# An attention scan with two expert layers: another order of the first pieces and loads, and other engines for the bonus and the low parts

## The chip, the core and the metric

The kernel runs on one core of one Trainium2 chip. The metric is the device time of one execution in microseconds (us). TensorE multiplies matrices, VectorE, ScalarE and GpSimd (POOL in the rows) work on elements, SyncE (SP) issues the transfers from and to HBM.

## The reference

Four sequences of 768 tokens, 8 heads of 48 columns. First a linear attention with a decaying state and a bonus `u` for the current token:

```
for t in range(S):
    cur = einsum('bhd,bhe->bhde', u[None] * kt, vt)
    y[:, :, t] = einsum('bhd,bhde->bhe', rt, state + cur)
    state = wt[..., None] * state + einsum('bhd,bhe->bhde', kt, vt)
```

Its 3072 rows of 384 go through a dense layer, `(max(h, 0) + alpha * min(h, 0)) @ w_out` with `h = x @ w_in` and 2048 inner columns, and then through eight experts of 1024 inner columns. Each row goes to the one expert whose normalised embedding has the largest product with it, and is scaled by its softmax weight.

## The kernel before

The tokens are cut into 24 tiles of 128 rows, tile n being chunk n // 4 of sequence n % 4, and three tiles make a block. The attention of a tile is written as eight pieces, `ATT[0..7]`, named `a<piece>.<tile>` in the table `PLAN`:

- `a0` (`att_p0`): a scan over the decays (L274), its inverse, and k times the result (L278), all on VectorE. `a1`: the second scan (L281), a square of the decays on ScalarE for a check (L283), and the bonus `att_u`, r times k times u on GpSimd (L289, L290).
- `a6` (`att_r`): r times the second scan (L295); from tile 4 on also the old state times its decay on GpSimd. `a7` (`att_d`): the bonus summed by head (L320) and multiplied with v (L322, tile `dv`).
- `a2`: k turned by TensorE (L330) and copied by ScalarE (`Kt`). `a3`: the scores of each head (L340), copied to `A` by ScalarE (L343) and masked by GpSimd (L344).
- `a4`: the new state (L354, L358, L360) and `y` (L366 and L369 on TensorE, L371 on VectorE, which adds `dv`). `a5`: `y` turned (L383) and split into a high part `xh` (ScalarE, L384) and a low part `xl` (VectorE, L385).

Matrices are multiplied as fp32r products of high and low parts, three for each product. The weights of the dense layer come as 64-bit words in 16 groups, `c<step>.<group>`: even groups are of w_in, odd ones of w_out. Step 0 is a shift on ScalarE (L197), step 1 two bit operations on VectorE (L199, L200), step 2 the high part on ScalarE (L211), step 3 the low part. The low part is one instruction on VectorE (L223), but for w_in's groups 2 to 5 (that is c4, c6, c8, c10, the list `LO_PE`) it is formed by TensorE (L219, L220) and copied by ScalarE (L221). `p0` and `p1` multiply w_out with the expert embeddings (`wt`, `wq`, L243 to L260). `s` normalises these embeddings (L879 to L886, tiles `en`, `ep`, `enT`) and casts the triangle `mf` to `trib`, and `w` is a run of idle products that keep TensorE busy.

`PLAN` is the order in which all engines get these pieces before the main loop. Then T counts 16 steps for each block: `l1` forms inner column group f = T mod 16 (nine products into `h_ps`, L408; then `m` on ScalarE and VectorE, L412 and L413, `gh`, L416, and `gl`, L422), `l2` takes the group of T - 2 to the outputs (L432). A step of block 0 also converts: step 0 of group T + 4, step 1 of T + 3, step 3 of T + 2. The pieces of a later tile begin at a T from the tables `AT1` and `AT`, and follow at distances `LAGS`. Each engine takes its instructions in exactly this order. There are two buffers for `h_ps`, and three PSUM buffers (`ps_a`) which the attention, the turned weights and the low parts share in turn. `LOADS` is the order of the first transfers, all on one queue of SyncE; a transfer is issued only when the eighth before it has landed.

Of the kernel before, what the change touches and what calls it, by code (L numbers as in the profile page):

```python
# [77 lines left out]
LOADS = [(0, "w"), "e", "id", (0, "rk"), "m", (0, "n"), "u", (1, "w"), (1, "rk"), (1, "n"), 0, (2,), 1, 2, 3]  # L78
PLAN = "a0.0 a1.0 s w6 a6.0 a2.0 a7.0 a3.0 a0.1 a1.1 a6.1 a4.0 a2.1 a7.1 a5.0 a3.1 c0.0 a0.2 a1.2 a6.2 a4.1 a2.2 a7.2 c1.0 c2.0 a5.1 a3.2 c0.1 c1.1 c3.0 c0.2 a4.2 c2.1 p0.0 c0.3 c1.2 a5.2 c3.1 c2.2"
# [15 lines left out]
def tile_main(ctx, tc, keep, x2d, tbl, att, w_in, w_out, alpha, u_row, u_col, emb, tau, w1, w2, cst, out):  # L95
# [95 lines left out]
    def conv(q, kind, g):  # L191

        t = stage[kind, g]
        lw, hw = t[:, :, 0], t[:, :, 1]
        lf = lw.bitcast(F32)
        if q == 0:
            ACT.activation(out=lf, in_=lw.bitcast(U32), func=AF.Copy, scale=-0.936 * 2.0 ** -51, bias=-2.0)  # L197
        elif q == 1:
            DVE.scalar_tensor_tensor(out=lw, in0=hw, scalar=3, in1=lw, op0=ALU.logical_shift_left, op1=ALU.bitwise_or)  # L199
            DVE.scalar_tensor_tensor(out=lw, in0=hw, scalar=0x3FFFFFFF, in1=lw, op0=ALU.bitwise_or, op1=ALU.bitwise_and)  # L200
        else:
            h, g0 = divmod(g, NG // 2)
            if kind == "in":
                hi, lo = (w[:, :, g0 * GW:(g0 + 1) * GW] for w in win[h])
            else:
                if h == len(wout):
                    wout_half()
                hi, lo = (w[:, g0 * GF:(g0 + 1) * GF, 0:DM] for w in wout[h])
            f3 = lf.rearrange("p (a b) -> p a b", a=(KD if kind == "in" else GF))
            if q == 2:  # L210
                ACT.activation(out=hi, in_=f3, func=AF.Copy, scale=-1.0)  # L211
            else:
                if (kind, g) in LO_PE:
                    m = 512 // hi.shape[2]
                    for a in range(0, hi.shape[1], m):
                        n = min(m, hi.shape[1] - a)
                        p = ps_a.tile([128, n, hi.shape[2]], F32, tag="a", name="lo_ps")
                        for b in range(n):
                            PE.matmul(out=p[:, b, :], lhsT=ident, rhs=f3[:, a + b, :], start=True, stop=False)  # L219
                            PE.matmul(out=p[:, b, :], lhsT=identr, rhs=hi[:, a + b, :], start=False, stop=True)  # L220
# [124 lines left out]

    def att_p4(n):
        c, b = divmod(n, B)
        r, v = rT(n, 0), nat(n, 2)
        if c < NCH - 1:
            up = ps_a.tile([128, HP, D], F32, tag="a", name="u_ps")  # L350
            for h in range(H):
                i = h % 2
                q = slice(64 * i, 64 * i + D)
                PE.matmul(out=up[q, h // 2, :], lhsT=Kt[:, h // 2, q], rhs=v[:, D * h:D * h + D], start=True, stop=True)  # L354
            for i in range(2):
                q = slice(64 * i, 64 * i + D)
                if c:
                    DVE.tensor_tensor(out=st[b][q], in0=up[q], in1=sbd[n % 2][q, :, D * i:D * i + D], op=ALU.add)  # L358
                else:
                    ACT.activation(out=st[b][q], in_=up[q], func=AF.Copy)  # L360
# [438 lines left out]
    if True:  # L799
        mf = sp.tile([128, 128], F32, tag="y", name="mf")  # L800
        for l in LOADS:
            if l == "e":
# [53 lines left out]
        def run(kind, *a):  # L856
# [474 lines left out]
```

## Time and profile before

| | us |
|---|---|
| median of 3 runs | 828.03 (827.75 to 828.66) |
| the profiled execution | 822.78 |
| its span, first to last instruction | 820.8 |
| TensorE busy | 788.3 (96%) |
| VectorE busy | 586.2 (71%) |
| ScalarE busy | 435.5 (53%) |
| GpSimd busy | 309.8 (38%) |

The shares are means over the whole span, in which the first 125 us, with the weights' conversion, differ from the rest. Durations below are from the profiled execution, whose time lies 5.25 us under the median.

### The profile page before, as it was taken

What the parts mean: (1) busy time and instruction counts of PE and PEld (TensorE: products, weight loads), DVE (VectorE), ACT (ScalarE), POOL (GpSimd) and SP (SyncE); (2) the same over time, 40 slices, a digit from 0 to 9 for tenths busy, and PEclk for the clock granted to TensorE, in tenths of its full rate; (3) what the DMA queues carried; (4) which work ended last, traced back from release to release, by engine and by line L of the source; (5) the groups of instructions that cost most, each with busy time, mean ns of one, the idle gap of its engine ahead of it and who ended that gap; (6) DMA issues with size and microseconds to landing.
All of it is one profiled execution on the core that took longest, in us unless ns stands there. A gap on an engine that the chain in (4) does not pass through costs nothing. (4 is left out here: it accounts for less than half of the span.)

```text
span 820.8 us, 16378 instructions
## 1 busy us (share of the span) xinstructions
PE 788.3 (96%) x6408; PEld 754.1 (92%) x6408; DVE 586.2 (71%) x1230; ACT 435.5 (53%) x845; POOL 309.8 (38%) x376
## 2 busy tenths in 40 slices
PE   6689999999999999999999999998899999999996
PEld 4579989999999999999999999897899999999996
DVE  6898886687586586676777674647987677768662
ACT  3667755345335444444533533436556676767662
POOL 4213322224124124124214212144466776767731
PEclk9689999999999999999999999999999999999998
DMA  8755512113324313113113100046756787676740
GB/s 316 257 164 210 178 69 88 68 53 114 123 82 149 123 58 98 69 68 97 70 68 97 69 1 30 31 168 203 183 207 210 272 272 261 223 278 225 257 174 32
DMA packets 31047, 117.26 MB, mean 143 GB/s; under 512 B 5693, under 2 KB 12829, under 8 KB 28145
## 3 DMA queue, kind: packets, MB, share of 16 engines
q0 software_dynamic: 13952, 59.86, 22.1%
q1 hardware_dynamic: 17008, 56.28, 20.0%
q8 instruction: 52, 0.85, 0.5%
q14 instruction: 35, 0.28, 0.2%
HBM read 101.79 MB, written 15.51 MB: 143 GB/s over the span
## 5 line engine op out<-in xcount | busy, mean ns | idle before, releaser
L412 ACT ACTIVATE m<-h_ps,al_sb 128x384 f32<-128x384 f32 x128 | 74.2, 580 | 125.9 <-PE h_ps L408 124.3
L413 DVE TENSOR_TENSOR m<-h_ps,m 128x384 f32<-128x384 f32 x128 | 71.0, 555 | 91.3 <-ACT m L412 89.9
L416 ACT ACTIVATE gh<-m 128x384 fp32r<-128x384 f32 x128 | 67.2, 525 | 113.3 <-DVE m L413 113.3
L422 DVE TENSOR_TENSOR gl<-m,gh 128x384 fp32r<-128x384 f32 x128 | 81.4, 636 | 36.2 <-ACT gh L416 36.1
L344 POOL TENSOR_SCALAR_AFFINE_SELECT A<-A 128x512 f32<-128x512 f32 x48 | 30.0, 648 | 178.0 <-ACT A L343 178.0
L685 POOL DMA_INDIRECT raw<-in_w,wix x64 | 67.5, 1054 | 49.1 <-DVE w0l L697 24.1
L727 PE MATMUL h_ps<-yh,w0h 128*128 128x256 f32 x264 | 77.0, 292 | 3.6 <-DVE g2l L732 3.6
L727 PE MATMUL h_ps<-yl,w0h 128*128 128x256 f32 x264 | 74.7, 283 | 0.3 <-DVE yl L718 0.3
L697 DVE TENSOR_TENSOR w1l<-raw,w1h 128x768 fp32r<-128x768 f32 x64 | 60.6, 953 | 19.8 <-ACT w1h L696 19.1
L727 PE MATMUL h_ps<-yh,w0l 128*128 128x256 f32 x264 | 74.3, 281 | 0.0
L408 PE MATMUL h_ps<-xh,win0h 128*128 128x384 f32 x192 | 69.6, 362 | 1.5 <-DVE m L413 1.5
L697 DVE TENSOR_TENSOR w0l<-raw,w0h 128x768 fp32r<-128x768 f32 x64 | 60.8, 959 | 12.5 <-ACT w0h L696 12.5
L408 PE MATMUL h_ps<-xh,win1h 128*128 128x384 f32 x192 | 67.8, 353 | 0.0
L408 PE MATMUL h_ps<-xl,win0h 128*128 128x384 f32 x192 | 65.6, 342 | 0.0
L432 PE MATMUL o_ps<-wout0l,gh 128*128 128x392 f32 x192 | 65.4, 340 | 0.0
L432 PE MATMUL o_ps<-wout1h,gl 128*128 128x392 f32 x192 | 65.4, 340 | 0.0
L432 PE MATMUL o_ps<-wout0h,gl 128*128 128x392 f32 x192 | 65.3, 340 | 0.0
L408 PE MATMUL h_ps<-xh,win0l 128*128 128x384 f32 x192 | 65.3, 340 | 0.0
L432 PE MATMUL o_ps<-wout0h,gh 128*128 128x392 f32 x192 | 65.3, 340 | 0.0
L432 PE MATMUL o_ps<-wout1h,gh 128*128 128x392 f32 x192 | 65.3, 340 | 0.0
L432 PE MATMUL o_ps<-wout1l,gh 128*128 128x392 f32 x192 | 65.2, 340 | 0.0
L408 PE MATMUL h_ps<-xh,win1l 128*128 128x384 f32 x192 | 64.9, 338 | 0.0
(284 smaller groups left out, 2274.6 us busy)
## 6 DMA issues: line engine op xcount, KB each, us to landing
ld<-in_att SPq DMA_DIRECT2D x21, 1348.5 KB, 6.8
stg<-in_w_in SPq DMA_DIRECT2D x24, 256.0 KB, 3.7
stg<-in_w_out SPq DMA_DIRECT2D x8, 768.0 KB, 4.5
x2d<-rows SPq DMA_DIRECT2D x24, 194.0 KB, 7.1
out<-zero SPq DMA_DIRECT2D x24, 192.0 KB, 7.2
att<-in_att SPq DMA_DIRECT2D x1, 1348.5 KB, 9.2
ld<-in_att SPq DMA_DIRECT2D x2, 576.0 KB, 6.7
ld<-in_att SPq DMA_DIRECT2D x2, 512.0 KB, 4.9
```

The lines of the kernel that those rows point to most:

```text
L344: POOL.affine_select(out=h, in_=h, pattern=[[0, HP], [1, CH]], compare_op=ALU.is_gt, fill=0.0, base=0, channel_multiplier=-1)
L408: PE.matmul(out=h, lhsT=w[:, k, :], rhs=x[:, k, :], start=(n == 0), stop=(n == 3 * KD - 1))
L412: ACT.activation(out=m, in_=h, func=AF.Copy, scale=al_sb[:, f:f + 1])
L413: DVE.tensor_tensor(out=m, in0=h, in1=m, op=ALU.min)
L416: ACT.activation(out=gh, in_=m, func=AF.Copy)
L422: DVE.tensor_tensor(out=gl, in0=m_t.pop((j, f)), in1=gh.bitcast(F32), op=ALU.subtract)
L432: PE.matmul(out=o_t[j][i], lhsT=g[:, s], rhs=w, start=(f == 0 and n == 0), stop=(f == KF - 1 and n == 2))
L685: POOL.indirect_dma_start(out=t, out_offset=None, in_=src, in_offset=idx(wix[:, h, COL[s]:COL[s] + 1]))
L697: DVE.tensor_tensor(out=lo, in0=a, in1=hi.bitcast(F32), op=ALU.subtract)
L727: PE.matmul(out=h, lhsT=w[:, k, :], rhs=x[:, k, :], start=(n == 0), stop=(n == 3 * KD - 1))
```

## The change

The first transfers stand in another order (`LOADS`): tile 2 is asked for in three parts ahead of the weights, the triangle `mf` and the row of u (`u_sb`) behind the first two groups of weights, the small column form of u (`u_bd`) ahead. `PLAN` is another order of the same pieces. For tiles 0 to 5 (`ND`) the natural rows of r and k are not loaded any more: VectorE multiplies the transposed r and k (`rk_prod`) and TensorE sums them with u by head (`dg_ps`); for tiles 0 and 1 (`AD`) ScalarE forms `dv`, head by head. All low parts of the weights are on VectorE. The embeddings are scaled and copied by ScalarE, and `trib` is cast by GpSimd. The state of tiles 0 to 3 is formed behind their `y`, the check on the decays of tiles 0 to 2 behind their `a5`. Tiles 6 to 8 begin at T = 16, 20 and 24, by `AT1`, where 6 to 8 had 12, 17 and 23.

```diff
-ND = range(0)
-AD = 0
+ND = range(6)
+AD = 2
-LO_PE = [('in', g) for g in range(2, 6)]
-LOADS = [(0, "w"), "e", "id", (0, "rk"), "m", (0, "n"), "u", (1, "w"), (1, "rk"), (1, "n"), 0, (2,), 1, 2, 3]
+LOADS = [(0, "w"), "e", "id", (0, "rk"), "v", (0, "n"), (1, "w"), (1, "rk"), (1, "n"), (2, "w"), (2, "rk"), (2, "n"), 0, 1, "m", "u", 2, 3]
-                if (kind, g) in LO_PE:
...
-                        ACT.activation(out=lo[:, a:a + n, :], in_=p, func=AF.Copy, scale=-1.0)
-                else:
-                    DVE.scalar_tensor_tensor(out=lo, in0=f3, scalar=-1.0, in1=hi.bitcast(F32), op0=ALU.mult, op1=ALU.subtract)
+                DVE.scalar_tensor_tensor(out=lo, in0=f3, scalar=-1.0, in1=hi.bitcast(F32), op0=ALU.mult, op1=ALU.subtract)
...
+        if n in ND:
+            DVE.tensor_tensor(out=rk_prod(n), in0=rT(n, 0), in1=rT(n, 1), op=ALU.mult)
         DVE.tensor_tensor(out=rT(n, 1), in0=rT(n, 1), in1=R1, op=ALU.mult)
...
-        if c < NCH - 1:
-            up = ps_a.tile([128, HP, D], F32, tag="a", name="u_ps")
...
+        if 0 < c < NCH - 1:
+            att_s(n)
...
+        if c == 0:
+            att_s(n)
...
+        if n < 3:
+            att_w(n)
...
+        POOL.tensor_copy(out=trib, in_=mf)
...
-            t0 = START[n] if j == 0 else 16 * (j - 1) + (AT1 if j == 1 else AT[BLK[j]])[n - B0[j]]
+            t0 = START[n] if j == 0 else 16 * (j - 1) + (AT1 if j < 3 else AT[BLK[j]])[n - B0[j]]
...
-                DVE.tensor_scalar(out=en, in0=en, scalar1=en2, scalar2=None, op0=ALU.mult)
+                ACT.activation(out=en, in_=en, func=AF.Copy, scale=en2)
...
-                DVE.tensor_copy(out=enT, in_=ep)
-                DVE.tensor_copy(out=trib, in_=mf)
+                ACT.activation(out=enT, in_=ep, func=AF.Copy)
```

GpSimd, from its last constants to the second tile. Before, it multiplies the bonus of each tile (L289, L290) between the masks of `A`:

```order
L830 IOTA tokid 128x24
L838 MEMSET oobt 128x216
L289 TENSOR_TENSOR ld<-ld 128x384
L290 TENSOR_TENSOR ld<-ld,u_sb 128x384
L344 AFFINE_SELECT A<-A 128x512 x2
L289 TENSOR_TENSOR ld<-ld 128x384
L290 TENSOR_TENSOR ld<-ld,u_sb 128x384
```

Now:

```order
L832 IOTA prow_122 128x1
L833 IOTA tokid 128x24
L841 MEMSET oobt 128x216
L842 CAST trib<-mf 128x128
L337 AFFINE_SELECT A<-A 128x512 x6
L249 TENSOR_TENSOR wout0l<-s_wp,wout0h 128x2x8 x3
```

The products are gone, the six masks of tiles 0 to 2 follow each other, and the cast of `mf` stands ahead of the first of them.

TensorE, from the `y` of tile 0 to the first `h_ps` (`att_130` is tile 2). Before:

```order
L369 MATMUL y_ps<-ld,A 64x48 x16
L330 MATMUL kt_ps<-ident,att_130 128x128 x4
L383 MATMUL t_ps<-ident,y 128x128 x3
L340 MATMUL a_ps<-att_130 128x128 x8
L354 MATMUL u_ps<-att_130,Kt 48x48 x8
L369 MATMUL y_ps<-att_130,A 64x48 x16
L243 MATMUL wt_ps_472<-ident,stg 128x128 x4
L243 MATMUL wt_ps_473<-ident,stg 128x128 x2
L383 MATMUL t_ps<-ident,y 128x128 x3
L254 MATMUL wq_ps<-enT,wt 32x8 x24
L408 MATMUL h_ps<-xh,win0h 128x384
```

Now, from the scores of tile 2:

```order
L333 MATMUL a_ps<-att_130 128x128 x8
L300 MATMUL dg_ps<-u_bd,att_130 128x2 x4
L383 MATMUL t_ps<-ident,y 128x128 x6
L323 MATMUL kt_ps<-ident,att_130 128x128 x4
L888 MATMUL ep<-ident,en 128x8 x3
L367 MATMUL y_ps<-att_130,A 64x48 x16
L346 MATMUL u_ps<-att_130,Kt 48x48 x8
L383 MATMUL t_ps<-ident,y 128x128 x3
L232 MATMUL wt_ps_506<-ident,stg 128x128 x4
L232 MATMUL wt_ps_507<-ident,stg 128x128 x2
L243 MATMUL wq_ps<-enT,wt 32x8 x24
L410 MATMUL h_ps<-xh,win0h 128x384
```

The turn of the embeddings (`ep`), which stood ahead of everything, now stands ahead of the `y` of tile 2; the `y` of tile 0 and 1 are turned together behind the scores of tile 2.

VectorE in T = 2 and the start of T = 3, from the second scan of tile 3. Before:

```order
L413 TENSOR_TENSOR m<-h_ps,m 128x384
L295 TENSOR_TENSOR ld<-ld,PS 128x512
L320 TENSOR_REDUCE dg<-ld 128x8
L322 TENSOR_TENSOR dv<-ld,dg 128x384
L422 TENSOR_TENSOR gl<-m,gh 128x384
L199 SCALAR_TENSOR_TENSOR stg<-stg 128x768
```

Now:

```order
L415 TENSOR_TENSOR m<-h_ps,m 128x384
L288 TENSOR_TENSOR ld<-ld,PS 128x512
L309 TENSOR_TENSOR dv<-ld,dg_ps 128x384
L212 SCALAR_TENSOR_TENSOR win0l<-stg,win0h 128x3x256
L424 TENSOR_TENSOR gl<-m,gh 128x384
L198 SCALAR_TENSOR_TENSOR stg<-stg 128x768
```

The reduction (L320) is gone, and the low part of group 4 (`win0l`, L212) has come between; the same holds for groups 6, 8 and 10 at T = 4, 6 and 8.

## Rows read from the trace of the kernel before

**Rows 1.** Busy time by stretches: window, length, then each engine, clock, DMA share, GB/s.

```profile
10.00:20.00 10.00, 8.18 (x82) 6.36 (x83) 7.26 (x13) 3.03 (x7) 4.84 (x5) 0.89 1.02 418
20.00:30.00 10.00, 6.07 (x81) 4.78 (x82) 9.23 (x13) 4.91 (x10) 4.43 (x4) 0.84 1.05 370
30.00:40.00 10.00, 7.59 (x120) 6.25 (x118) 7.19 (x10) 7.67 (x14) 1.22 (x2) 0.50 0.39 148
50.00:60.00 10.00, 7.06 (x38) 5.86 (x36) 9.62 (x14) 7.81 (x16) 0.23 (x1) 1.00 0.66 209
120.00:140.00 20.00, 20.00 (x179) 19.30 (x178) 12.99 (x23) 10.21 (x22) 5.10 (x7) 1.00 0.34 118
```

**Rows 2.** Timeline of VectorE to 44 us: start, duration, operation, idle time before it.

```profile
6.97 0.69 DVE L278 TENSOR_TENSOR ld<-ld,PS 128x512 f32<-128x512 f32 x1 [1.55 <-DMA ld<-in_att]
...
12.69 1.23 DVE L274 TENSOR_TENSOR_SCAN PS<-ld,anew 128x520 f32<-128x520 f32 x1
...
16.11 0.94 DVE L295 TENSOR_TENSOR ld<-ld,PS 128x512 f32<-128x512 f32 x1
19.18 0.56 DVE L371 TENSOR_TENSOR y<-y_ps,dv 128x384 f32<-128x384 f32 x1 [2.14 <-PE y_ps L369]
...
36.33 0.95 DVE L223 SCALAR_TENSOR_TENSOR win0l<-stg,win0h 128x768 fp32r<-128x768 f32 x1
...
43.95 0.56 DVE L413 TENSOR_TENSOR m<-h_ps,m 128x384 f32<-128x384 f32 x1 [0.18 <-ACT m L412]
```

**Rows 3.** DMA issues of 14 to 16 us: size, and us from issue to landing.

```profile
stg<-in_w_out SPq DMA_DIRECT2D x1, 768.0 KB, 11.1
...
al_sb<-in_alpha SPq DMA_DIRECT2D x1, 8.0 KB, 10.9
```

**Rows 4.** Timeline of GpSimd to 23 us.

```profile
8.60 1.00 POOL L289 TENSOR_TENSOR ld<-ld 128x384 f32<-128x384 f32 x1 [5.39 <-DMA ld<-in_att]
...
22.90 1.22 POOL L344 TENSOR_SCALAR_AFFINE_SELECT A<-A 128x512 f32<-128x512 f32 x2 [3.32 <-ACT A L343]
```

**Rows 5.** Timeline of TensorE to 40 us.

```profile
13.23 1.72 PE L340 MATMUL a_ps<-ld 64*128 64x128 f32 x16
...
33.90 2.32 PE L369 MATMUL y_ps<-att,A 128*64 128x48 f32 x32
...
39.89 0.69 PE L408 MATMUL h_ps<-xh,win0h 128*128 128x384 f32 x1
```

**Rows 6.** Timeline of ScalarE to 32 us.

```profile
16.83 0.64 ACT L360 ACTIVATE st<-u_ps 48x192 f32<-48x192 f32 x2
...
26.66 0.72 ACT L283 ACTIVATE att<-att,wmid 128x512 f32<-128x512 f32 x1 [2.54 <-DVE PS L281]
...
31.38 0.89 ACT L211 ACTIVATE win0h<-stg 128x768 fp32r<-128x768 f32 x1 [2.74 <-DVE stg L200]
```

**Rows 7.** Timeline of VectorE from 45 to 100 us.

```profile
45.76 0.17 DVE L276 TENSOR_SCALAR ip_all<-PS 128x4 f32<-128x4 f32 x1
...
65.19 0.56 DVE L413 TENSOR_TENSOR m<-h_ps,m 128x384 f32<-128x384 f32 x1 [1.89 <-ACT m L412]
...
67.02 0.80 DVE L276 TENSOR_SCALAR ip_all<-PS 128x4 f32<-128x4 f32 x1
...
99.67 0.56 DVE L371 TENSOR_TENSOR y<-y_ps,dv 128x384 f32<-128x384 f32 x1
```

**Rows 8.** Timeline of TensorE from 65 to 126 us.

```profile
65.97 0.61 PE L219 MATMUL lo_ps<-stg,ident 128*128 128x256 f32 x2
...
67.68 0.87 PE L243 MATMUL wt_ps<-ident,stg 128*128 128x128 f32 x6
...
101.23 0.49 PE L383 MATMUL t_ps<-ident,y 128*128 128x128 f32 x3
...
107.95 1.16 PE L340 MATMUL a_ps<-ld 64*128 64x128 f32 x14 [1.39 <-ACT s_wp L258]
...
125.72 0.60 PE L330 MATMUL kt_ps<-ident,ld 128*128 128x128 f32 x4
```

More of the change, by code (lines that the diff above doesn't have):

```diff
@@ L212, in conv @@
             else:
-                if (kind, g) in LO_PE:
[L214 to L220, printed above, removed]
-                        ACT.activation(out=lo[:, a:a + n, :], in_=p, func=AF.Copy, scale=-1.0)
-                else:
-                    DVE.scalar_tensor_tensor(out=lo, in0=f3, scalar=-1.0, in1=hi.bitcast(F32), op0=ALU.mult, op1=ALU.subtract)
+                DVE.scalar_tensor_tensor(out=lo, in0=f3, scalar=-1.0, in1=hi.bitcast(F32), op0=ALU.mult, op1=ALU.subtract)
                 del stage[kind, g]
@@ L270, in att_p0 @@
     def att_p0(n):
-        if n in ND:
-            DVE.tensor_tensor(out=rk_prod(n), in0=rT(n, 0), in1=rT(n, 1), op=ALU.mult)
         w = ld_t[n][:, LD - LW:LD]
@@ L281, in att_p1, with att_w @@
         DVE.tensor_tensor_scan(PS[:, LW:], ld_t[n][:, LD - LW:LD - 2], anew[:, 0:LW - 2], 0.0, ALU.mult, ALU.add)
+        if n > 2:
+            att_w(n)
+        if n not in ND:
+            att_u(n)
+    def att_w(n):
         steps = wT(n)[:, :, 2:CW]
         ACT.activation(out=steps, in_=steps, func=AF.Square, bias=wmid, accum_out=dev[:, n:n + 1])
-        if n not in ND:
-            att_u(n)
     def att_u(n):
@@ L344, in att_p3, with att_s @@
             POOL.affine_select(out=h, in_=h, pattern=[[0, HP], [1, CH]], compare_op=ALU.is_gt, fill=0.0, base=0, channel_multiplier=-1)
+    def att_s(n):
+        c, b = divmod(n, B)
+        v = nat(n, 2)
+        up = ps_a.tile([128, HP, D], F32, tag="a", name="u_ps")
+        for h in range(H):
+            i = h % 2
+            q = slice(64 * i, 64 * i + D)
+            PE.matmul(out=up[q, h // 2, :], lhsT=Kt[:, h // 2, q], rhs=v[:, D * h:D * h + D], start=True, stop=True)
+        for i in range(2):
+            q = slice(64 * i, 64 * i + D)
+            if c:
+                DVE.tensor_tensor(out=st[b][q], in0=up[q], in1=sbd[n % 2][q, :, D * i:D * i + D], op=ALU.add)
+            else:
+                ACT.activation(out=st[b][q], in_=up[q], func=AF.Copy)
     def att_p4(n):
@@ L348, in att_p4 @@
         r, v = rT(n, 0), nat(n, 2)
-        if c < NCH - 1:
-            up = ps_a.tile([128, HP, D], F32, tag="a", name="u_ps")
[L351 to L360, printed above, removed]
+        if 0 < c < NCH - 1:
+            att_s(n)
         yp = ps_a.tile([128, DM], F32, tag="a", name="y_ps")
@@ L385, in att_p5 @@
         DVE.tensor_tensor(out=lo, in0=tp, in1=hi.bitcast(F32), op=ALU.subtract)
+        if n < 3:
+            att_w(n)
         del ld_t[n]
@@ L805, in tile_main @@
                 SP.dma_start(out=u_sb, in_=u_row.to_broadcast([128, DM]))
+            elif l == "v":
                 SP.dma_start(out=u_bd, in_=u_col.rearrange("p (h i) -> p h i", h=HP))
```

2 lines of the change are left out of this document (1 added, 1 removed).

## The prediction

> **What bounds the kernel now.** I began with the table of busy time by stretches [rows 1]. From 120 us on TensorE is busy 20.00 of 20 us at a granted clock of 1.00, and in the timeline it runs without a wait from there to the end of the dense layers. A change that touches only the first 125 us is therefore worth what it moves one event: the start of T = 16, where TensorE begins block 1. Before, that boundary stands at 125.72 us, with the first transpose of tile 6 [rows 8]. Ahead of it two other things bind. In 50 to 60 us VectorE is busy 9.62 of 10 us while TensorE has gaps (7.06 of 10) [rows 1], and the stretches around are alike: there the conversion of the weights on VectorE sets the pace. In 30 to 40 us no engine reaches 8 of 10, and TensorE's granted clock is 0.50, its 1.2 GHz level, after it had waited [rows 1]: the first three tiles are a chain from engine to engine. So I follow VectorE through three anchors: its first `m` of block 0 (L413, 43.95 us) [rows 2], the `y` of tile 4 (L371, 99.67 us) [rows 7], and the boundary at 125.72.
>
> **Term A, up to the first `m`.** I walk the new order with durations of before. Tile 0 waits for its r and k, which stand in the same place in the queue and land at 6.97 us [rows 2]. A tile costs VectorE about 4 us (12.69 to the end of L295 at 16.11 without its slow part), and the new r-times-k product 0.6 more (as L278) [rows 2]. Tile 0 is through at 10.0 and tile 1 at 14.6, since the loads of tile 1 now stand 640 KB nearer to the front. TensorE has the scores of tile 0 by 11.8 (1.72 from 10.1) [rows 5], ScalarE copies them by 12.9 (as L343).
>
> Then comes the step on which most hangs. On GpSimd the cast `trib<-mf` now stands ahead of the first masks, and `mf` is loaded behind tile 2 and two weight groups. After r and k of tile 0 the queue holds, by the shapes in the code, 3,725 KB up to and with `mf`. At the 418 GB/s of 10 to 20 us (408 KB per us) that is 9.1 us, at the 370 GB/s of 20 to 30 us 10.3 us [rows 1]: it lands between 16.1 and 17.3, and I take 17.0. A small transfer does not pass large ones here: the 8 KB of `al_sb`, asked for between 14 and 16 us behind 768 KB of weights, took 10.9 us, the weights 11.1 [rows 3]. The Trainium skill (DMA: Bandwidth & Descriptors, Queues, rings and completion order) says that each DMA engine takes descriptors in ring order, but also that completion is not first-in first-out for an issuing engine. By the second half `mf` could land early; no run here shows that, and it is the second rival below.
>
> The cast costs GpSimd some 0.45 us (no row; between nothing and the 1.00 of the three times larger product), the two masks 1.22 [rows 4]: tile 0 is masked at 18.8, not at 14.1. Behind it wait `y` of tile 0 on TensorE (2.0 us, since TensorE has idled again; tile 2 took 2.32 in the stretch of clock 0.50) [rows 5], `y` on VectorE, all of tile 2 on VectorE, and the scores of tile 1, whose second PSUM buffer that `y` frees. VectorE is idle from 14.6 to 20.8; `y` of tile 0 starts there at 20.8 against 19.18 [rows 2]. From there: tile 2 to 25.9, two bit steps of group 0 to 27.8 (each 0.95, as the low part L223 of the same size) [rows 2], `y` of tile 1 to 28.3, which frees the buffer for the scores of tile 2: to 30.1. ScalarE copies them (1.05, to 31.2), then works in order through xh of tile 0, the square of its decays (0.72), the high part of group 0 (0.89) [rows 6] and xh of tile 1 (0.45 each): 33.65. VectorE: xl 34.1, group 1 36.0, norm of the embeddings 36.35. Only now can ScalarE scale them (36.8) and TensorE turn them (37.35), and `y` of tile 2, whose inputs were ready at 32, stands behind that turn on TensorE. It ends at 39.65 at half clock; u and transposes to 41.45, xl of tile 2 43.0, high part of group 1 44.05, copies of the turned w_out 45.0, its products 45.85. The first `h_ps` matmul then starts at 45.85, against 39.89 [rows 5]. VectorE has the low part of group 1 and the bits of groups 2 and 3 (44.95 to 48.75) and reaches `m` at 49.2: **A = +5.2**. The ScalarE bonus of tiles 0 and 1 (nine small ACTIVATEs a tile, of 48 columns and fewer; two of 192 columns took 0.64 [rows 6], so at most 0.32 each and I take 0.2) is hidden even at 0.32: `dv` of tile 0 is ready at 15.9, before 20.8, that of tile 1 at 27.5, before 27.8; without that cover the 1.8 of the second would be late in full. Ends of A: 3.6 (`mf` at 16.1, TensorE at full clock) and 6.6 (`mf` at 18, half clock in all of tile 2).
>
> **Term B, VectorE from `m` to `y` of tile 4.** Before, 43.95 to 99.67: 55.7 us. Four low parts come from TensorE and ScalarE to VectorE (groups 4, 6, 8, 10), each 0.95 long [rows 2], of which the next start overlaps some 0.08: +3.5. Products for tiles 3 and 4: +1.2. One bonus reduction falls away: -0.6. GpSimd no longer multiplies r, k and u for these tiles; beside it L276 took 0.80 at T = 4 and at T = 8, against 0.17 at 45.76 [rows 7]: -1.3. VectorE waits seven times in that stretch, 5.4 us in all; two of the waits, at T = 4 (65.19) and T = 8, are of 1.89 and for ScalarE's `m` [rows 7]. There ScalarE has the copies of a tile ahead of its `m` whatever TensorE does: after VectorE's last `m` it needs 0.45 (gh) + 0.85 (high part) + 0.4 (two small copies) + 0.83 (shift) + 0.55 + 1.05 (copies of the tile) + 0.5 (`m`) = 4.6 us, VectorE 0.87 + 0.47 + 1.9 = 3.2 in between, so 1.4 stays at each: -5.4 + 2.8. Sum 55.9: **B = +0.2**; at least -2.6 (no wait is left), at most +1.0 (the small waits stay). The start of tile 6 does not fall into this stretch.
>
> **Term C, from `y` of tile 4 to the boundary.** The transpose of tile 4 waits for that `y`. Before, TensorE was busy with older work and took it at 101.23, 1.56 us after `y` began, then needed 24.5 us to 125.72, with a wait of 1.39 at 107.95 [rows 8]. Now TensorE has worked off its older work and waits: it takes the transpose 0.55 us after `y` starts. Tile 6 leaves block 0, so VectorE's steps at T = 12 to 14 are short and the wait goes: 23.1 us. **C = -2.4**, and -1.0 if the wait stays. In block 1 tile 6 adds some 6 us to VectorE, which there is busy 12.99 of 20 us [rows 1], and its two TensorE steps only move from T = 16 to T = 20: no cost.
>
> **Sum.** 5.2 + 0.2 - 2.4 = +3.0 us. The profiled execution, 822.78 us with its span of 820.8, would become 825.8. It lies 5.25 under the median of 828.03; on the median's scale the forecast is **831.0**. This measurement can tell about 0.2%, 1.7 us, from no change. The forecast's own range is 829.7 to 833.2; the ends of the terms together give -1.4 to +6.6.
>
> **The rivals.**
> *VectorE's waits vanish.* B at -2.6 gives +0.4: 828.4, no change. For it: ScalarE has two copies of low parts fewer ahead of it every other T, so its `m` may come sooner. Against it: the waits stand exactly where ScalarE copies a tile's scores.
> *`mf` lands early.* If its 64 KB pass the weights and land by 13 us, tile 0 is masked at 14, `y` follows VectorE's tile 1 directly, and A is 6.0 less: 5.2 - 6.0 + 0.2 - 2.4 = -3.0, 825.0, faster. It decides from the point where `mf` lands before the copies of the scores (12.9). Against it stands `al_sb` [rows 3].
> *TensorE stays the bound of block 0.* From its first `h_ps` at 45.85 the old 85.8 us to the boundary lose four low parts of 1.71 (65.97 to 67.68 [rows 8]), the 2.94 us of gaps in 50 to 60 [rows 1] and the 1.39, and gain three bonus products of some 0.5: 76.2, so the boundary at 122.0, -3.7: 824.3. The Trainium skill (Perfetto Trace Analysis, Identifying the Most-Contended Engine) tells to optimise the engine of highest occupancy first, which over this span is TensorE; by that rule all of it would be gained. The windows of block 0 speak for VectorE instead.
> *The clock falls in block 0.* TensorE now waits there; at half clock 18 matmuls take some 6 us, above VectorE's 5.0 a step, and three such steps give +4: 835. Against it: 7.06 busy of 10 us went with a clock of 1.00 [rows 1].
>
> **Numbers.** Forecast 0.50; waits vanish 0.20; `mf` early 0.14; TensorE bound 0.10; clock 0.06. Slower is forecast and clock, 0.56; same 0.20; faster 0.24. The range takes in the case of an early `mf` and the upper bounds of A and B: 824.8 to 834.5, which leaves out the last two cases, 0.16.
>
> **What would show it.** Step by step: GpSimd's first mask at 17.5 us and not 13; `y` of tile 0 on VectorE near 20.8; a wait of TensorE's `ep` for ScalarE's `en` until near 37; the first `h_ps` near 45.9; waits of 1 to 2 us for `m` at T = 4 and T = 8; the boundary near 128.7 with TensorE dense from the transpose of tile 4 on. The forecast is wrong if `mf` is there by 14 us, if the first `h_ps` starts before 42, or if TensorE has no gaps between 60 and 105 us.

## The result, and the profile after

| | before | changed |
|---|---|---|
| median, us | 828.35 (827.75 to 829.02, 4 runs) | 837.46 (836.3 to 838.34, 4 runs) |
| profiled execution, us | 822.78 | 836.3 |
| TensorE busy, us | 788.3 | 795.1 |
| mean granted clock of TensorE | 0.985 | 0.968 |

The ratio is 1.0109, 95% interval 1.0091 to 1.0126: the change makes the kernel 9.1 us slower. Forecast were 3.0 us, with 6.5 as the upper end of the range. The sign was right, the size was not.

TensorE is busy for 7 us more, although the low parts were taken from it. I followed the start of each step T (the first of the nine matmuls of `h_ps`) through both timelines. The changed kernel is behind by 5.98 us at T = 0 (45.87 against 39.89), by 7.76 at T = 15 (130.21 against 122.45) and by 9.42 at T = 34 (209.59 against 200.17). From there to T = 126, the last step but one of the dense layers, the distance stays at 9.41 to 9.42. So all that matters lies ahead of 210 us. The profiled executions differ by 13.5 us, but what comes behind that differs from one execution to the next, and the medians differ by 9.1. (From the start of T = 127 to the last instruction it is 264.0 us before and 266.7 changed; in the runs below it is 264.2 to 267.0, and 264.2 and 264.3 stand in two kernels with the changed start, f3_fill and f4_start.)

Busy time by stretches in the changed kernel (window, length, then PE, PEld, DVE, ACT, POOL, clock, DMA share, GB/s), to be read beside [rows 1]:

```profile
10.00:20.00 10.00, 5.75 (x55) 5.28 (x56) 4.57 (x7) 3.94 (x12) 1.47 (x3) 0.50 1.04 395
20.00:30.00 10.00, 10.00 (x110) 9.25 (x110) 8.14 (x11) 5.86 (x17) 2.16 (x2) 0.50 0.27 91
50.00:60.00 10.00, 7.50 (x88) 6.83 (x86) 9.86 (x15) 5.79 (x13) 0.00 (x0) 0.95 0.29 84
60.00:70.00 10.00, 8.70 (x97) 8.17 (x98) 9.58 (x14) 7.84 (x15) 0.73 (x2) 0.83 0.61 189
110.00:120.00 10.00, 10.00 (x107) 9.44 (x106) 7.60 (x12) 6.26 (x14) 1.66 (x3) 0.88 0.14 58
```

From 10 to 30 us the granted clock is 0.50, the 1.2 GHz level, where before it was 0.89 and 0.84. From 20 to 30 us TensorE is busy all the time at that level, so there it is not an engine that waits; that it sets the pace there is likely but not shown (g3_fill_start, below, was inconclusive). And in block 0, where it was 1.00 from 50 us on, the clock now falls again and again.

GpSimd, timeline of the changed kernel, for [rows 4]:

```profile
17.05 0.29 POOL L842 CAST trib<-mf 128x128 bf16<-128x128 f32 x1 [13.85 <-DMA mf<-in_cst]
17.30 1.22 POOL L337 TENSOR_SCALAR_AFFINE_SELECT A<-A 128x512 f32<-128x512 f32 x2
```

TensorE in the start, for [rows 5]:

```profile
12.03 1.86 PE L300 MATMUL dg_ps<-u_bd,ld 128*128 128x2 f32 x8
17.99 2.32 PE L367 MATMUL y_ps<-ld,A 128*64 128x48 f32 x32 [4.09 <-POOL A L337]
...
37.88 0.48 PE L888 MATMUL ep<-ident,en 8*128 8x8 f32 x3 [4.53 <-ACT en L885]
...
45.87 0.69 PE L410 MATMUL h_ps<-xh,win0h 128*128 128x384 f32 x1
```

The cast waits 13.85 us for `mf`, TensorE 4.09 us for the mask behind it and later 4.53 us for the scaled embeddings. Both waits were forecast, at these places.

VectorE, for [rows 2] and [rows 7]:

```profile
20.42 0.56 DVE L369 TENSOR_TENSOR y<-y_ps,dv 128x384 f32<-128x384 f32 x1 [5.71 <-PE y_ps L367]
...
49.77 0.56 DVE L415 TENSOR_TENSOR m<-h_ps,m 128x384 f32<-128x384 f32 x1 [0.52 <-ACT m L414]
...
71.66 0.56 DVE L415 TENSOR_TENSOR m<-h_ps,m 128x384 f32<-128x384 f32 x1 [1.88 <-ACT m L414]
...
95.34 0.56 DVE L415 TENSOR_TENSOR m<-h_ps,m 128x384 f32<-128x384 f32 x1 [1.90 <-ACT m L414]
...
107.43 0.56 DVE L369 TENSOR_TENSOR y<-y_ps,dv 128x384 f32<-128x384 f32 x1
...
108.97 0.55 DVE L309 TENSOR_TENSOR dv<-ld,dg_ps 128x384 f32<-128x384 f32 x1
```

These give the prediction's terms: A is 49.77 - 43.95 = +5.8 (forecast +5.2), B 107.43 - 49.77 = 57.7 against 55.7, +1.9 (forecast +0.2), and C runs from 107.43 to the boundary at 133.48: 26.05, as long as before (forecast -2.4).

TensorE at T = 11, for [rows 8]:

```profile
106.04 0.95 PE L300 MATMUL dg_ps<-u_bd,ld 128*128 128x2 f32 x8
107.50 1.05 PE L232 MATMUL wt_ps<-ident,stg 128*128 128x128 f32 x6 [0.51 <-PE dg_ps L300]
109.57 0.90 PE L383 MATMUL t_ps<-ident,y 128*128 128x128 f32 x3 [1.02 <-DVE dv L309]
110.12 0.67 PE L410 MATMUL h_ps<-xh,win1h 128*128 128x384 f32 x1
110.59 0.52 PE L410 MATMUL h_ps<-xl,win1h 128*128 128x384 f32 x1
...
133.48 0.34 PE L410 MATMUL h_ps<-xh,win0h 128*128 128x384 f32 x1
```

`y` of tile 4 is ready from 108 us on, but its transpose starts at 109.57. It needs one of the three `ps_a` buffers, and one is held by the bonus product of tile 5 (106.04) until VectorE's `dv` has read it at 108.97, behind `y`, an `m` and a scan's product. Of the 1.6 us, 0.55 are TensorE's own older work (`wt_ps`, until 108.55) and 1.02 are the wait for `dv`. After this wait the matmuls follow each other by 0.32 us where 0.175 is usual: the nine of T = 11 take 2.86 us where before it was 1.83.

### The profile page after: what moved, and what is told of

Read it like the earlier page. It is cut to its first block, busy times and chain, and to the rows that moved or that the text cites. A ratio compares the mean times of both kernels' runs of the same rounds, so it can differ in the third digit from the quotient of the medians.

```text
span 834.2 us, 16396 instructions
## 1 busy us (share of the span) xinstructions
PE 795.1 (95%) x6420; PEld 761.0 (91%) x6420; DVE 583.7 (70%) x1229; ACT 436.8 (52%) x857; POOL 296.0 (35%) x365
## 4 chain that ended last, share of the span: by engine, by line
PE 78%; DVE 9%; issue 5%; ACT 3%; DMA 2%; POOL 1%; SPq 0%; POOLq 0%; DVEq 0%; ACTq 0%
PE h_ps L410 23%; PE o_ps L434 21%; PE h_ps L729 9%; PE o_ps L755 9%; PE a_ps L333 3%; PE y_ps L367 3%; PE o_ps L787 2%; PE h_ps L765 2%; PE y_ps L364 2%; DVE m L415 1%; PE u_ps L346 1%; PE t_ps L383 1%; PE kt_ps L323 1%; PE x_ps L718 1%; DVE PS L261 1%
```

## The experiments

Below, a "slow step" is one whose nine matmuls of `h_ps` take over 2.4 us (1.7 to 2.0 otherwise; the first three steps are not counted). "T0 to T15" runs from the first matmul of step 0 to that of step 15, in the profiled execution. The us are the ratio's, of 828; each kernel was timed beside the kernel before on its own chip. The intervals are 1 to 2.5 us to either side. (What the expectations call T = 32 is T = 34 by the code's count.) The columns from "first `h_ps`" on are of one execution each. With the same start, the first `h_ps` came between 45.79 and 47.01 us (changed, e2, e3, e4, f3, f4), and with block 0 as before T0 to T15 took 82.56, 82.72, 84.08 and 84.47 us (before, f4_start, g1_before_fill, g2_mended). A difference of less than 2 us in these two columns, or one slow step, therefore shows nothing by itself. T15 to T34 repeats better: 77.7 to 77.8 in the eight kernels in which tile 6 begins as before.

| kernel | ratio to before (95%) | us | first `h_ps` | T0 to T15 | T15 to T34 | slow steps: T, us |
|---|---|---|---|---|---|---|
| before | 1 | 0 | 39.89 | 82.56 | 77.72 | none |
| changed | 1.0109 (1.0091 to 1.0126) | +9.1 | 45.87 | 84.34 | 79.38 | 3: 2.79, 7: 2.90, 11: 2.86 |
| e1_mf_early | 1.0077 (1.0059 to 1.0094) | +6.4 | 41.91 | 84.57 | 79.22 | 3: 2.94, 7: 3.01, 11: 2.92 |
| e2_nd3 | 1.0158 (1.0135 to 1.0182) | +13.1 | 46.03 | 87.74 | 79.61 | 3: 2.90, 8: 3.24, 12: 2.83 |
| e3_lope | 1.0117 (1.0096 to 1.0137) | +9.7 | 46.98 | 85.73 | 78.41 | 3: 3.22 |
| e4_tile6 | 1.0087 (1.0069 to 1.0106) | +7.2 | 47.01 | 85.74 | 77.78 | 3: 3.22, 7: 3.23, 11: 3.06 |
| e5_mf_s | 1.0058 (1.0044 to 1.0073) | +4.8 | 40.57 | 85.34 | 80.68 | 3: 3.22, 7: 2.86, 11: 3.05 |
| b1_lo_dve | 1.0053 (1.0038 to 1.0069) | +4.4 | 39.99 | 87.04 | 77.78 | 3: 3.23, 8: 3.23, 12: 2.48 |
| b2_dg | 1.0025 (1.0013 to 1.0036) | +2.1 | 39.67 | 83.98 | 77.78 | none |
| b3_block0 | 1.0038 (1.0023 to 1.0054) | +3.1 | 38.77 | 84.23 | 78.40 | 3: 3.23 |
| f1_lo_idle | 1.0029 (1.0012 to 1.0045) | +2.4 | 40.07 | 84.46 | 77.78 | 3: 2.63 |
| f2_tile6_alone | 1.0020 (1.0004 to 1.0035) | +1.7 | 39.53 | 84.12 | 79.09 | 12: 2.84 |
| f3_fill | 1.0091 (1.0070 to 1.0113) | +7.5 | 45.79 | 83.41 | 78.40 | 3: 2.76 |
| f4_start | 1.0071 (1.0052 to 1.0090) | +5.9 | 45.97 | 82.72 | 77.71 | none |
| g1_before_fill | 1.0000 (0.9983 to 1.0017) | 0 | 39.93 | 84.08 | 77.77 | 12: 2.61 |
| g2_mended | 0.9979 (0.9962 to 0.9996) | -1.7 | 37.46 | 84.47 | 77.75 | 12: 2.88 |
| g3_fill_start | 1.0102 (1.0075 to 1.0128) | +8.4 | 43.79 | 85.35 | 78.42 | 3: 2.70, 7: 3.22 |

**One part of the changed kernel undone.** First the late triangle:

```diff
-LOADS = [(0, "w"), "e", "id", (0, "rk"), "v", (0, "n"), ..., 0, 1, "m", "u", 2, 3]
+LOADS = [(0, "w"), "e", "id", (0, "rk"), "v", "m", (0, "n"), ..., 0, 1, "u", 2, 3]
```

> The changed kernel with one thing undone: the triangle mf is asked for ahead of v of tile 0, as before, and not behind two groups of weights. Theory (the late triangle sets the start): GpSimd's first mask near 13 us where it stood at 17.3, y of tile 0 on VectorE near 15 where it stood at 20.4, and the first m of block 0 some 6 us earlier, near 44, with all behind it moved as one: about 831.5 us. Rival (the new order of the pieces sets the start, above all the embeddings' turn that waits for ScalarE): y of tile 0 comes early all the same, but the first m at most 2 us earlier, 48 or later, and the time 835.5 or more.

The first mask came at 12.37 us and `y` of tile 0 at 16.04; the first `m` at 45.81, 4.0 earlier, not 6. Between the two theories: the late `mf` is the larger part of the start's loss, but behind it TensorE then met the next wait, as long as in the changed kernel (its timeline):

```profile
33.91 0.48 PE L888 MATMUL ep<-ident,en 8*128 8x8 f32 x3 [4.53 <-ACT en L885]
```

Then the bonus of tiles 3 to 5:

```diff
-ND = range(6)
+ND = range(3)
```

> The changed kernel with the bonus of tiles 3 to 5 as before (natural r and k loaded, GpSimd's products, VectorE's sum), and only tiles 0 to 2 by TensorE. Theory (the bonus product of tile 5 holds a PSUM buffer until VectorE's dv, the turn of tile 4 waits for it, and TensorE runs the next step at half clock): the wait of t_ps for dv at T = 11 is gone, and with it the half clock of that step, 2.6 us in all; VectorE gains three products of 0.6 and loses two sums of 0.55 and what GpSimd's products slow; the boundary at T = 16 near 131, the time near 835. Rival (VectorE sets the pace there and those waits of TensorE are hidden): the boundary stays within 0.7 us of 133.5, the time at 837 to 838.

Neither: it is 4 us slower still. The wait of t_ps for `dv` is gone, and other waits came, longer ones: at T = 8 TensorE's timeline shows

```profile
90.29 0.48 PE L333 MATMUL a_ps<-ld 64*128 64x128 f32 x2 [1.01 <-DVE xl L385]
92.17 2.07 PE L333 MATMUL a_ps<-ld 64*128 64x128 f32 x14 [1.39 <-ACT s_wp L247]
```

and the step behind took 3.24 us. So the theory that the bonus product of tiles 3 to 5 is what costs in block 0 fell for the changed kernel.

The low parts of groups 4, 6, 8 and 10 back on TensorE and ScalarE (the list `LO_PE` and its branch, as in the kernel before):

> The changed kernel with the low parts of groups 4, 6, 8 and 10 formed by TensorE and copied by ScalarE, as before. Theory (VectorE paces block 0 from its first m to y of tile 4): four low parts of 0.87 leave VectorE, that stretch shrinks from 57.7 to 54 to 55.5 us, and the boundary comes 2 to 3.5 us earlier: 834 to 835.5 us. Rival (TensorE, with the bonus products and its waits for PSUM buffers, has no room left for 6.8 us more): the stretch does not shrink, the time is 837 or more.

The rival held: no gain. The slow steps at T = 7 and 11 are gone, but the stretch from the first `m` to `y` of tile 4 grew, from 57.7 to 59.3 us (50.88 to 110.16).

Tile 6 as before:

```diff
-(AT1 if j < 3 else AT[BLK[j]])
+(AT1 if j == 1 else AT[BLK[j]])
```

> The changed kernel with tiles 6 to 8 begun at T = 12, 17 and 23 as before. In the profiles the start of each step lay 7.8 us behind the kernel before at T = 16 and 9.4 behind at T = 32, so block 1 lost 1.65 us more. Theory (that loss comes from tile 6's pieces in block 1): the lag no longer grows in block 1, and since TensorE waits for nobody at T = 12 to 14 block 0 does not grow: about 835.8 us. Rival (the loss in block 1 is a chance of one execution, such as the 0.7 us for which y waited for nothing that the profile shows): 837 to 838 us, or more if VectorE's steps at T = 12 to 14 become longer again.

The theory held for block 1: T15 to T34 takes 77.78 us, as before. The time is 1.8 us below the changed kernel's, though the two intervals overlap. In the one profile the same start and block 0 took 2.5 us longer than the changed kernel's, so that T = 34 stands at 210.53, not before 209.59; the medians do not show that.

**One part of the change put into the kernel before.** The low parts on VectorE (`LO_PE = []`):

> The kernel before with one part of the change alone: the low parts of groups 4, 6, 8 and 10 on VectorE. Theory (the prediction's working: VectorE gets four times 0.87, its waits for m at T = 4 and T = 8 take up part of that, and TensorE is 6.8 us freer): the stretch from the first m to y of tile 4 goes from 55.7 to 56 to 57, the time is 827 to 829 us against 827 to 828 before. Rival (the waits for m do not shrink, because ScalarE has the copies of a tile ahead of its m): the full 3.5 us arrive, 830 to 831.5.

The rival's time, but not for its reason alone: three slow steps, and TensorE's timeline at T = 3 shows the longest wait of all runs ahead of the first (issue means that the profile shows nothing that it waited for):

```profile
54.91 1.53 PE L243 MATMUL wt_ps<-ident,stg 128*128 128x128 f32 x6 [4.08 <-issue]
56.09 0.67 PE L408 MATMUL h_ps<-xh,win0h 128*128 128x384 f32 x1
56.56 0.52 PE L408 MATMUL h_ps<-xl,win0h 128*128 128x384 f32 x1
```

The bonus of tiles 3 to 5 on TensorE (`ND = range(3, 6)`):

> The kernel before with one part of the change alone: the bonus of tiles 3 to 5 by TensorE, without their natural r and k. Theory (the product dg holds a PSUM buffer until VectorE's dv, and TensorE stands and then runs a step at half clock): a wait of t_ps for dv of 1 us or more and a step of nine matmuls of 2.8 us in place of 1.85 after it; the time is 1 to 2.5 us above before. Rival (undoing this part in the changed kernel cost 3 us, so it is a gain: no products by GpSimd beside VectorE, smaller loads, two reductions fewer): the time is 1 to 2 us below before.

2.1 us slower, as the theory says, but without its mechanism: no wait of t_ps for `dv`, no slow step. What the profile does show is that TensorE is as dense as before (39.97 busy of the 40 us from 60 to 100) and that the 24 matmuls of the bonus take 2.4 us of it, while its waits from T = 0 to T = 15 fall from 4.8 to 3.9: 1.4 us more in all. At T = 34 the profile is 1.3 us behind the kernel before's.

Both, and tile 6 (`AT1 if j < 3`):

> The kernel before, with its old start (PLAN, LOADS, tiles 0 to 2 as they were), and all parts of the change that act in blocks 0 and 1: the low parts on VectorE, the bonus of tiles 3 to 5 by TensorE, tiles 6 to 8 begun at T = 16, 20 and 24. Theory (the parts add up, the start apart): from the first m to T = 32 it takes 3.6 us longer than before, as in the changed kernel (159.8 us against 156.2), so about 3.6 us above before. Rival (those losses come from the late start, which puts VectorE and TensorE in another phase to each other): within 1.5 us of before.

The parts of blocks 0 and 1 cost 3.1 us with the old start too (1.9 to 4.5). They are no child of the late start. And the waits of the changed kernel for `dv` are here as well, 1.26 us at T = 7 and 1.02 at T = 11, but the clock did not fall behind either; TensorE's timeline at T = 11:

```profile
102.94 0.55 PE L383 MATMUL t_ps<-ident,y 128*128 128x128 f32 x3 [1.02 <-DVE dv L316]
103.24 0.42 PE L408 MATMUL h_ps<-xh,win1h 128*128 128x384 f32 x1
```

**Is it TensorE's idleness or VectorE's work?** In the next kernel VectorE forms the low parts, and TensorE still makes its products for them, unread:

```diff
                             PE.matmul(out=p[:, b, :], lhsT=identr, rhs=hi[:, a + b, :], start=False, stop=True)
-                        ACT.activation(out=lo[:, a:a + n, :], in_=p, func=AF.Copy, scale=-1.0)
-                else:
-                    DVE.scalar_tensor_tensor(...)
+                DVE.scalar_tensor_tensor(...)
```

> The kernel before with the low parts of groups 4, 6, 8 and 10 on VectorE, as in b1_lo_dve, but TensorE still forms its products for them, which nobody reads. So VectorE has the same work as in b1_lo_dve and TensorE the same as before; only ScalarE's eight copies fall away. Theory (what those low parts cost is TensorE's: without the products it stands 2.5 to 4 us at T = 3, 8 and 12 and runs the next step at half clock): those three steps take 1.85 us again in place of 2.5 to 3.2, and the time is 827.5 to 829.5. Rival (VectorE's 3.5 us more are the cost): as b1_lo_dve, 830.5 to 832.

2.4 us above before: between the two. More work on TensorE, nothing less on VectorE, and T0 to T15 fell from 87.04 to 84.46 us; TensorE's waits in it fell from 11.5 to 5.9 us (4.8 before). Of the two slow steps at T = 8 and 12 none is left. The intervals of the two times just overlap, so that unread products give back half of the loss is likely, not certain.

Tile 6 alone (`AT1 if j < 3` in the kernel before):

> The kernel before with tiles 6 to 8 begun at T = 16, 20 and 24 and nothing else of the change. Theory (the prediction's working for this part: VectorE's steps at T = 12 to 14 get short, a wait of 1.4 us of TensorE goes, block 1 has room): 0.5 to 1.5 us below before. Rival (what block 1 lost in the changed kernel, 1.65 us, comes with this part): 0.5 to 1.5 us above before.

The rival held, 1.7 us slower (0.3 to 2.9). T15 to T34 takes 79.09 us. And at T = 12 TensorE's wait for `s_wp`, of which the prediction said that it goes, is there unchanged; in this execution the clock fell behind it:

```profile
107.62 1.71 PE L340 MATMUL a_ps<-ld 64*128 64x128 f32 x14 [1.39 <-ACT s_wp L258]
109.25 0.69 PE L408 MATMUL h_ps<-xh,win1h 128*128 128x384 f32 x1
109.74 0.52 PE L408 MATMUL h_ps<-xl,win1h 128*128 128x384 f32 x1
```

In [rows 8] the same instruction waited the same 1.39 us and took 1.16. The fall is not the work of tile 6's new start: g1_before_fill, whose code from T = 0 on is that of the kernel before, has it too,

```profile
107.97 1.94 PE L340 MATMUL a_ps<-ld 64*128 64x128 f32 x14 [1.41 <-ACT s_wp L258]
109.84 0.69 PE L408 MATMUL h_ps<-xh,win1h 128*128 128x384 f32 x1
```

and f4_start and f1_lo_idle, with the same wait of 1.4 us, do not. So it differs from one execution to the next, and the sure sign of tile 6's cost is block 1 alone.

Idle products ahead of the bonus product, in the changed kernel:

```diff
-            dp = ps_a.tile([128, H, 1], F32, tag="a", name="dg_ps")
+            dp = ps_a.tile([128, 512], F32, tag="a", name="dg_ps")
+            if n > 2:
+                for _ in range(10):
+                    PE.matmul(out=dp[:, 128:512]..., lhsT=oneb, rhs=oneb..., start=True, stop=True)
+            dp = dp[:, 0:H].rearrange("p (h o) -> p h o", o=1)
```

> The changed kernel with ten idle products (of constants, 128x384 each, about 1.6 us together) ahead of the bonus product of tiles 3, 4 and 5, in the part of the same PSUM buffer that the product leaves free. They fill most of the time for which TensorE stood at T = 3, 7 and 11; nothing waits for them that is not waiting already. Theory (the half-clock steps behind those waits are part of the loss): the steps at T = 3, 7 and 11 take 1.85 us in place of 2.8 to 2.9, and the time is 1 to 2 us below the changed kernel's, that is 1.007 to 1.009 of before. Rival (those steps lie beside VectorE's work, or the clock falls all the same): within 0.5 us of the changed kernel, 1.0105 to 1.0115 of before.

The theory held by the steps, and its time, 1.5 us less, is at the edge of what was expected, with intervals that overlap; at T = 34 the profile is 2.0 us ahead of the changed kernel's (207.60 against 209.59). Only half of that comes from block 0: at T = 15 it is 1.0 ahead (129.20 against 130.21), the rest is a wait of the changed kernel at 208.63 that is not in this profile. T = 7 and 11 take 1.8 us again, and each gives about 0.5 of the 1.0 us by which it is shorter; at T = 3, where 1.65 us of the wait were left, the step stayed slow. TensorE's timeline at T = 11:

```profile
105.51 1.80 PE L301 MATMUL dg_ps<-oneb 128*128 128x384 bf16 x10
...
109.12 0.55 PE L387 MATMUL t_ps<-ident,y 128*128 128x128 f32 x3 [0.21 <-DVE dv L313]
109.42 0.42 PE L414 MATMUL h_ps<-xh,win1h 128*128 128x384 f32 x1
109.68 0.33 PE L414 MATMUL h_ps<-xl,win1h 128*128 128x384 f32 x1
```

The 1.8 us of idle products delay nothing: `h_ps` starts at 109.42, where it was 110.12. That they held the clock is not shown by this run alone: b3_block0 had no slow step at T = 7 and 11, and g3_fill_start none at T = 11, with the waits for `dv` and without idle products in block 0.

**The start.** Alone, with blocks 0 and 1 as before (the changed kernel with `ND = range(3)`, `LO_PE` and the old start of tile 6):

> The start of the change alone: PLAN, LOADS, the bonus of tiles 0 to 2 by TensorE and the embeddings on ScalarE as in the changed kernel; tiles 3 to 5, the low parts of groups 4 to 10 and the start of tile 6 as before. Theory (the parts add up: the changed kernel is 9.1 us slower, the other parts alone 3.1): first m near 50 us, from there to T = 32 as before 156.2, the time 6 us above before. Rival (the late start also puts the engines of block 0 in another phase to each other, as the run with tiles 3 to 5 undone suggests, which was 3 us slower still): from the first m to T = 32 over 158 us, the time 8 us or more above before.

The theory held to 0.2 us: first `m` at 49.97, from there to T = 34 156.4, and 5.9 us in all. Block 0 as before has no slow step.

`mf` early and `s` early, in the changed kernel:

```diff
-PLAN = "a0.0 a1.0 w6 a2.0 ... c1.1 s c3.0 ..."
+PLAN = "a0.0 w6 s a1.0 a2.0 ... c1.1 c3.0 ..."
```

> The changed kernel with mf asked for early, and with the embeddings' step s right behind the first scan of tile 0 and not behind the bit operations of group 1. In the run with mf early alone TensorE stood 4.5 us before the embeddings' turn (ep), while the scores of tile 2 were already masked. Theory (what is left of the late start is that wait): y of tile 2 some 4 us earlier, the first m of block 0 at 41 to 42.5 us (43.95 before the change, 45.8 with mf early alone), and the time another 3 to 4 us lower than 833.35: 829 to 830.5. Rival (VectorE's bit operations of groups 2 and 3 hold the first m): it comes at 44.5 or later, the time at 832 or more.

Neither quite: the first `m` at 44.47, 1.3 earlier than with `mf` alone, the time 1.6 us less, with intervals that overlap. TensorE's wait for the embeddings is gone, `y` of tile 2 started at 32.03 where it was 34.33; but the granted clock was still 0.50 from 10 to 20 us and 0.67 from 20 to 40.

Idle products in the changed start (`w4` ahead of `a3.0`, `w10` ahead of `a4.0`, `w16` ahead of `s`):

> The changed kernel with idle products in its start: four ahead of the scores of tile 0, ten ahead of y of tile 0, where TensorE waited 4.1 us for the mask, sixteen ahead of the embeddings' turn, where it waited 4.5 us. Order and loads are those of the changed kernel. Theory (TensorE at half clock binds the start between the first mask and the turn of tile 1): at 2.4 GHz the work from 18 to 33.4 us takes 4 to 6 us less, and the first m comes 2 to 4 us earlier than 49.8: the time 2 to 4 us below the changed kernel's, 1.006 to 1.0085 of before. Rival (mf, and VectorE's work up to s, hold the start whatever the clock): the first m at 48.8 or later, the time within 1 us of the changed kernel's.

Inconclusive: the first `m` came 2.1 us earlier, as the theory says, and T = 34 is 2.0 earlier (207.56 against 209.59), but half of that goes with a wait at 211.80, behind T = 34, and at T = 126 nothing of it is left (9.38 behind the kernel before, where the changed kernel is 9.42); the time is 0.6 us less, with 2 us of interval. They could not hold the clock: ten of them took 2.0 us, TensorE then waited 3.66 us more for the late mask, and from 20 to 30 us the clock was 0.59.

The same in the kernel before (`w8` ahead of `a5.1`, `w5` ahead of `a4.2`):

> The kernel before with idle products (of constants, 128x384) where TensorE waits in its start: eight ahead of the turn of y of tile 1, where it waited 2.8 us, and five ahead of y of tile 2, where it waited 1.7 us. Theory (its start too is lengthened by the clock, 0.50 from 30 to 40 us): the first h_ps 2 to 4 us before 39.9, but the first m of block 0 waits for VectorE's bit operations and gains less, 0.5 to 2 us; the time 0.5 to 2 us below before. Rival (VectorE holds the start of the kernel before): the first m within 0.5 us of 43.95, the time within 0.2% of before.

The rival held: first `m` at 43.99, no difference in time, and VectorE waits only 0.18 us ahead of that `m`, as before. But though the clock from 30 to 40 us rose from 0.50 to 0.82, the first `h_ps` came no earlier (39.93, its nine matmuls at half clock as before), so the run does not show what an earlier `h_ps` would give there.

All three mended (`mf`, `s` and idle products), blocks 0 and 1 as before:

> The changed start with its three causes mended (mf early, s right behind the first scan, idle products where TensorE waits), and tiles 3 to 5, the low parts and tile 6 as before. Theory (the late triangle, the late turn of the embeddings and the clock are the whole of the start's 5.8 us): the first m at 41 to 43 us against 43.95 before, from there to T = 32 as before 156.2, the time 1 to 3 us below before. Rival (the new order itself costs, with VectorE's bit operations of four groups ahead of the first m): the first m at 44 or later, the time at before or up to 2 us above.

First `m` at 41.73 us, first `h_ps` at 37.46 and at the full level, 1.86 us for its nine matmuls; ratio 0.9979. This is the one version that beats both kernels, by 1.7 us (0.3 to 3.1). From the first `m` to T = 34 it takes 157.95, not 156.2: here T = 12 is a slow step, as in g1_before_fill.

## Why the prediction was right or wrong

*The sum by parts.* The start alone costs 5.9 us (f4_start), the parts of blocks 0 and 1 with the old start 3.1 (b3_block0): 9.0 of the 9.1 measured. With intervals of 1 to 2 us on each, that close a match is luck, but that the two halves add up is shown. Of the 3.1, the new start of tile 6 alone costs 1.7 (f2_tile6_alone; 1.8 by e4_tile6), which leaves 1.4 for low parts and bonus. In the two profiles the boundary lies 7.76 us late where 3.0 were forecast, 0.6 of the difference in term A, 1.7 in B and 2.4 in C, and 1.66 more come in block 1, for which the sum had nothing. The forecast was near for the start; it is the rest that failed.

*What bounds the kernel was misread.* "... the stretches around are alike: there the conversion of the weights on VectorE sets the pace." That fits 50 to 60 us alone. In the kernel before the windows behind it are:

```profile
60.00:70.00 10.00, 10.00 (x112) 9.26 (x112) 7.97 (x13) 7.73 (x16) 4.52 (x5) 1.00 0.37 112
70.00:80.00 10.00, 10.00 (x145) 9.45 (x144) 9.43 (x14) 7.74 (x17) 2.02 (x3) 1.00 0.66 246
80.00:90.00 10.00, 9.96 (x109) 9.05 (x109) 7.33 (x11) 7.48 (x16) 3.75 (x5) 1.00 0.51 179
90.00:100.00 10.00, 10.00 (x156) 9.59 (x155) 9.60 (x15) 7.67 (x15) 2.72 (x4) 1.00 0.47 145
```

TensorE was busy for 39.96 of these 40 us, VectorE for 34.33. So TensorE's own work and waits had to stand in the sum too. From T = 0 to T = 15 the changed kernel's TensorE loses 7.3 us of products for low parts; but it gains 3.0 of bonus products, its waits grow from 4.8 to 7.4, its `h_ps` matmuls take 3.3 longer, and with small items it needs 1.8 us more.

*Term A was right*, nearly step by step: `mf` at 17.05 (17.0), first mask at 17.30 (17.5), `y` of tile 0 at 20.42 (20.8), `ep` at 37.88 (37.35), first `h_ps` at 45.87 (45.85), first `m` at 49.77 (49.2). That `mf` came behind the weights agrees with the Trainium skill (DMA: Bandwidth & Descriptors, Queues, rings and completion order) in its first half, ring order; no run here shows a case of the second. One reason was off: TensorE was taken for an engine that waits, with the half clock in tile 2 alone, but it runs at 0.50 from 10 us on; the sum came out near all the same because the mask, for which TensorE waited 4.09 us, held tile 0. And undoing the late `mf` gave back 4.0 us of the first `m` and 2.7 of time, not the 6.0 that the rival had, because `ep` waited next.

*Term B was mis-sized*, +1.9 in place of +0.2. Its waits came where they were forecast, at T = 4 and T = 8, but at 1.88 and 1.90 us, as long as before, not 1.4; with two small ones they make 4.6 us where 2.8 stood in the sum. ScalarE needs 5.06 us from VectorE's `m` of T = 3 (its end at 66.57) to the end of its own of T = 4 (71.63), not 4.6. I also missed the third product, that of tile 5 at T = 8 (+0.6), and the second reduction that falls away (-0.55). That is 0.2 + 1.8 + 0.6 - 0.55 = 2.05. The upper bound of +1.0 was too low by its own rows: the five small waits that might stay were 1.6 us together, which gives +1.8.

*Term C failed.* "It takes the transpose 0.55 us after `y` starts": it took 2.14 us (107.43 to 109.57). TensorE had not worked off its older work, and the bonus product, for which no cost was put in the sum, held a PSUM buffer for 1.02 us more. "The wait goes: 23.1": from the transpose to the boundary it took 23.9, with one step 1.0 longer at half clock. The wait at T = 12, which I took for tile 6's, stays when tile 6 alone goes (f2_tile6_alone); in the changed kernel those of T = 11 stand in its place. "Its two TensorE steps only move: no cost" failed too: in all nine kernels with the new start of tile 6 T15 to T34 takes 78.4 to 80.7 us, in all eight with the old one 77.7 to 77.8. That this part costs is shown. The profiles show in part how. In all nine, 0.7 us are lost between T = 15 and T = 33 (73.0 to 73.1 us, against 72.3 to 72.4 in the other eight), without a wait of TensorE over 0.17 us: the same products in another order take that much longer. The rest is one wait of 0.3 to 2.0 us in the `y` of tile 9 or before its turn, behind T = 33, in eight of the nine (0.73 us at 208.63 in the changed kernel, without a releaser in the profile) and in none of the others. Why it comes stays open.

*The rivals.* VectorE's waits did not vanish, and `mf` was not early. TensorE as the bound of block 0 fell: the kernel freed of four low parts on TensorE got 4.4 us slower (b1_lo_dve), and half of that came back when TensorE did them unread (f1_lo_idle). By the Trainium skill (Perfetto Trace Analysis, Identifying the Most-Contended Engine) the engine of highest occupancy comes first, though it calls TensorE's busy time a poor measure of how near that engine is to its limit; over the span that engine is TensorE, and here taking work from it and giving it to VectorE lost time. The falling clock, put at 0.06, was in part what happened: three slow steps, each some 1.0 us longer. In f3_fill, without two of them, T = 15 comes 1.0 us earlier, so about half of each was on the path.

*What stays open.* The parts of blocks 0 and 1 do not add up one by one: low parts 4.4, bonus 2.1 and tile 6 1.7 alone, 3.1 together. With low parts and bonus both, VectorE loses two reductions and TensorE has the bonus products in its gaps, which fits, but was only argued. The 2.1 us of b2_dg fit the 2.4 us of bonus products on a TensorE that has hardly a gap from 60 to 100 us, but no run tested that. And when the clock falls behind a wait and when not is not known from these runs.

## What to carry to other kernels

Where two engines pace each other, what an engine off the path does in its gaps can matter: work taken from it can lengthen its waits, with a risk of half-clock steps behind them, and unread products in a gap may be worth more than a shorter queue. Read every window of a stretch before one engine is called the bound. A small product that is put into a rotating PSUM buffer must be costed by how long its reader lets it wait, not by its own duration. And when a late load is mended, look for the next wait behind it before the whole of the loss is put down to it: here 6.0 were expected and 4.0 came.

## What the runs showed of the hardware

The same wait does not always cost the same. At T = 12 TensorE waited 1.39 to 1.41 us for the same instruction (`s_wp`) in eight kernels. In the kernel before, f1_lo_idle and f4_start the nine matmuls behind it took 1.84 us; in b1_lo_dve, g1_before_fill, e2_nd3, f2_tile6_alone and g2_mended they took 2.48 to 2.88. Block 0's code is the same in before and g1_before_fill, so one execution's slow step cannot be put down to an edit. And a busy TensorE is not a fast one: from 20 to 30 us the changed kernel's was busy 10.00 of 10 us, with small products of 2, 48 and 128 columns, at a granted clock of 0.50 throughout.
